# A spectral-filter and MLP block on one core: stores grouped, DRAM copies laid out by block, one bias spread on chip, and a new order of the engines

## The chip, the core and the metric

The kernel runs on one core of a Trainium2 chip. The core has TensorE (PE in the profile; its weight loads are PEld), VectorE (DVE), ScalarE (ACT), GpSimd (POOL) and SyncE (SP), which here issues most of the DMA transfers. Transfers can also be issued from ScalarE's instruction queue. The metric is the device time of one launch in microseconds, as the median of several runs.

## The reference

One block is computed forward and backward in bf16, for 2048 rows of 512 values. The forward pass, cut to what matters:

```
mod = (silu(c) @ w_mod) -> six rows sa, ca, ga, sb, cb, gb
h   = layernorm(x) * (1 + ca) + sa
y   = irfft2( rfft2(h) * (w_r + i w_i) )          # filter of 2048 x 257
x   = x + ga * y
h   = layernorm(x) * (1 + cb) + sb
x   = x + gb * ( relu(h @ w1 + b1)^2 @ w2 + b2 )  # 512 -> 1792 -> 512
```

The kernel returns this x and, for a given grad_out, the gradients of x, w_r, w_i, w1, b1, w2, b2, c and w_mod. In the kernel they are out_0 (x), out_1 (gradient of x), out_2 and out_3 (filter gradients, 2048 x 257), out_4 to out_7 (w1, b1, w2, b2), out_8 (c, 512 values) and out_9 (w_mod).

## The kernel before, in words

The Fourier transforms are matmuls with constant cosine and sine blocks. The launch runs through these stages; the times are those of the profiled execution.

- **0 to 50 us.** x is loaded into x_sb (load_x, four reads of 512 KB), the mod rows are formed (L736), the first layernorm runs (L767 to L784; n1 is stored to n1_dram) and the first transform (L294, L295) is made. As filler, TensorE computes grad_out times w2 transposed (back_products, L840); gT and w2T come by transposing DMAs.
- **50 to 86 us.** The second transform (spec_f23, L318 and L332) gives eight groups gi of the spectrum. Each group is multiplied by the filter (cmul, L415 to L418) and stored to xs_dram for the backward pass. lg_part makes a transposed constant LG out of LF by transposing DMAs. The inverse starts with spec_g1 (L352, L355; its results are evacuated into utcs at L360 on VectorE and L362 on ScalarE).
- **86 to 112 us.** spec_g2 and spec_g3 (L372, evacuated as Tsb at L374; L382) give y row by row. x is loaded again (x1, L911), the second layernorm (from L928 on, L943) gives h2, which a transposing DMA turns into h2T. b2, broadcast to all partitions in grow (L886), goes into x + gb * b2.
- **112 to 265 us.** The MLP, forward and backward, in blocks of rows: L1005 (h), L1034 (its output) and the gradient through them. w1T comes by four transposing DMAs (L1138).
- **265 to 340 us.** The backward spectrum: spec_f23 again, and ew_b, which multiplies by the conjugate filter and, in place in the reloaded xs tile Xb, forms the filter gradient. The filter gradient is stored at L1322 as 34 pieces, those of out_2 from SyncE, those of out_3 from ScalarE. Filler on TensorE are 32 units of the gradient of w1 (grad_w1, L1276; evacuated L1281). GMod.emit (L453 to L474) makes a block of the gradient of w_mod: a matmul (L460), an evacuation gmbc (L462), scaled copies gwm (L469, L471) and their stores (L474). LGb is read back (L1328) and grad_out is read into g_sb (L1341). After that comes the second spec_g1.
- **338 to 412 us.** The second spec_g2 and spec_g3 and the first layernorm's backward (L1421 to L1451) give out_1. Filler are units of the gradient of w2 (grad_w2, L1360; evacuated as gw at L1361, stored at L1362), whose left operands hn are transposing reads of h_dram (L1196). The last mod gradients and out_8 (PE transpose L1484, copy L1486, store L1487) end the launch.

What each engine does, and in which order, is written out by hand: a table ORDER lists for each of the five engines its instructions in the order in which they are to run, and set_order chains them. SyncE's list is thus one queue of DMA issues: an issue whose data or buffer isn't ready holds back all behind it. Every DMA takes one of eight completion semaphores in turn and waits for the transfer that had the semaphore before it, so at most eight are in flight.

SBUF tiles come from pools, and a pool that is opened late takes over memory of one that was released: the tiles of rows (x1, n2rows, y, Tsb) lie where the spectrum tiles Xs were, and the tiles of the last stage where Xb was.

Of the kernel before, what the change touches and what calls it, by code (L numbers as in the profile page):

```python
# [11 lines left out]
FP32 = mybir.dt.float32  # L12
# [6 lines left out]
D = 512  # L19
# [421 lines left out]
class GMod:  # L441
# [7 lines left out]
    def load(self, jc, pool):  # L449
        cs = slice(jc * D, (jc + 1) * D)  # L450
        self.tiles[jc] = [pool.tile([P, 2, D], BF16, name="wmc", bufs=4) for _ in range(2)]
        for dc in range(0, 4, 2):
            self.tc.nc.sync.dma_start(self.tiles[jc][dc // 2], self.wm_view[:, dc:dc + 2, cs])  # L453

    def emit(self, jc, q, row, pool, ppool, nbuf=2, last=False):
# [8 lines left out]
        for dc in range(0, 4, 2):  # L464
            wmc = self.tiles[jc][dc // 2]
            gwm = pool.tile([P, 2, D], BF16, name="gwm", bufs=nbuf)
            for i in range(2):
                if i == 0 or last:
                    nc.scalar.activation(gwm[:, i, :], gmbc, AF.Copy, scale=self.scf[:, dc + i:dc + i + 1])  # L469
                else:  # L470
                    nc.vector.tensor_scalar(gwm[:, i, :], gmbc, self.scf[:, dc + i:dc + i + 1], None, op0=ALU.mult)  # L471
                nc.vector.scalar_tensor_tensor(out=junk, in0=wmc[:, i, :], scalar=K["onef"], in1=gmbc, op0=ALU.mult, op1=ALU.mult,
                                               accum_out=self.gsc[:, jc, dc + i:dc + i + 1])
            nc.sync.dma_start(self.out9_view[:, dc:dc + 2, cs], gwm)  # L474
# [5 lines left out]
        "0-17 106 135-146 18-21 151-154 147-150 159-162 26-27 22-25 28-29 155-158 30-35 167-170 163-166 36-37 175-178 171-174 "  # L480
        "42-43 38-39 44-45 40-41 183-186 179-182 86-89 50-53 187-190 46-49 191-194 107-110 195-198 58-59 54-57 199-202 60-61 "
        "90-93 203-210 62-63 66-69 94-97 64-65 215-218 98-101 211-214 70-73 102-105 74-77 219-222 78-79 111-126 80-85 223-226 303 "
        "127-134 304-311 227-234 312-319 235-238 320-321 324-325 322-323 239-242 328 243-246 326-327 329-331 336-337 332-333 "
        "338-339 334-335 251-254 247-250 340-343 352-353 344 354-355 345-351 255-258 356-359 259-262 360-369 372-373 370-371 "
        "374-391 267-270 448-479 263-266 484-487 480-483 271-278 500-501 488-489 512-515 502-503 279-282 504-505 283-286 490-493 "
        "516-517 494-495 506-511 496-499 287-290 524-525 542-545 530-531 518-519 536-537 526-529 520-521 546-547 522-523 532-533 "
        "548-549 538-539 534-535 540-541 560-565 578-579 550-553 580-583 566-567 554-555 572-575 556-559 568-569 576-577 570-571 "
        "291-294 584-587 295-298 588-592 299-302 593-597 392-395 607-610 606 396-399 652-655 611 400-403 665-668 664 404-407 "
        "678-679 677 680-681 408-415 691-692 416-419 598 690 693-694 420-423 599-604 848 605 424-427 849-850 428-431 851 432-439 "
        "861-862 440-443 695 612 863 613-619 444-447 860 864 620-627 640-643 628-635 882-883 636-639 884-885 644-651 656-663 "  # L490
        "669-676 682-689 696-811 895 812-819 896 820-831 840-847 897 852-859 865-868 898 832-839 873-880 869-872 881 886-894 "
        "900-913 899 1052 914-955 1053 956-983 1054 984-997 1055 998-1023 1065 1024-1027 1064 1028-1031 1066-1068 1032-1035 "
        "1044-1051 1056-1063 1086-1087 1069-1072 1088 1073-1076 1089 1036-1043 1077-1084 1090-1093 1099-1100 1085 1094-1097 1101 "
        "1098 1102 1104-1117 1103 1118-1231 1252 1248-1249 1232-1239 1256-1263 1253 1264-1271 1254 1280-1283 1304-1310 1300-1303 "
        "1296-1299 1255 1250 1284-1287 1240-1247 1288-1295 1326-1332 1276-1277 1315-1321 1278-1279 1337-1343 1251 1348-1354 1272 "
        "1370-1376 1273-1274 1359-1365 1275 1322 1381-1387 1311 1392-1405 1312 1323-1324 1313-1314 1325 1406-1419 1344 1333-1334 "
        "1345-1346 1335-1336 1347 1436-1449 1355 1366 1356 1367 1357-1358 1368-1369 1450-1463 1377 1388-1391 1378-1380 1504-1519 "
        "1420-1421 1424-1425 1422-1423 1426-1429 1432-1435 1430-1431 1464-1487 1537-1552 1520 1488-1489 1500-1501 1490-1492 "
        "1496-1499 1493 1502-1503 1494-1495 1553-1616 1521-1525 1529-1530 1533-1534 1526 1531-1532 1535-1536 1527-1528 1617-1632 "
        "1634-1640 1642-1643 1633 1646-1649 1641 1650-1665 1644-1645 1682-1683 1666-1681 1694-1697 1684-1687 1690-1691 1688-1689 "  # L500
        "1692-1693 1698-1729 1743-1744 1730-1735 1745-1746 1739-1740 1736-1738 1741-1742 1763-1778 1780-1782 1792-1793 1783-1785 "
        "1788-1789 1794-1795 1790-1791 1786 1747-1762 1787 1796-1811 1828 1836-1837 1829 1779 1838-1839 1830-1831 1840-1841 1832 "
        "1842-1843 1833-1835 1812-1827 1864-1867 1860-1863 1868-1885 1890-1891 1886-1889 1896-1899 1892-1895 1914-1915 1900-1903 "
        "1916-1921 1904-1909 1926-1927 1922-1923 1928-1929 1910-1913 1932-1935 1930-1931 1924-1925 1936-1937 1844-1859 1968-1971 "
        "1938-1939 1972-1973 1956-1957 1940-1941 1950-1951 1942-1943 1958-1959 1944-1945 1960-1965 1952-1955 1946-1947 1966-1967 "
        "1974-1975 1948-1949 1976-1979 1984-1985 1980 1986-1987 1981-1983 1988-2004 2006-2008 2005 2010-2013 2009 2014-2029 2048 "
        "2052-2053 2049 2054 2050 2055 2051 2046-2047 2030-2045 2082 2078 2073 2079 2083-2084 2080 2085 2072 2081 2056-2071 2118 "
        "2128 2124 2129 2125-2126 2130 2127 2119 2131 2086-2101 2158 2154 2159 2155-2156 2102-2117 2160 2157 2208-2223 2074-2077 "
        "2120-2123 2150-2153 2149 2161 2132-2148 2200 2162-2177 2201 2204-2206 2202 2194 2203 2195 2207 2178-2193 2224-2240 "
        "2250-2251 2246 2241 2247-2249 2252-2269 2196-2199 2242-2245 2308-2309 2271 2276-2291 2270 2292-2307 2272-2275 2326-2333 "  # L510
        "2310-2325 2350 2334-2349 2367 2351-2366 2368-2416"
    ),
    "ACT": (
        "0 2 1 3 8 5 7 17 4 13 16 6 50 9 51 10 52 20 11-12 53 14 55 54 15 56 19 23-24 57 18 37 42 38 58 21-22 59 27 25 60 26 "
        "30-31 61 44 39 28-29 34 40 62 43 32 41 45 33 63 77 35-36 46 64 79 47 65 80 66 48 81 67 82 84 83 49 68 85-88 69 89-94 "
        "104-107 109 108 70-71 110-111 72-73 113 112 78 74 116 115 114 119 117-118 120 75 121-122 76 123 127 131 130 95 146 132 "
        "150 149 96 124 157 153 97 125 98 126 161 99 160 128 100 129 133 186 101 134-135 102 162 136 103 137-139 190 140-145 "
        "147-148 151-152 197 154 159 158 155-156 163-168 172 169-171 173 178 175 179 174 180-183 176 184-185 177 188 187 189 191 "
        "193 192 198-199 201 200 202 194-196 203 205 204 206-207 209 212 208 211 210 213 226 218 215 219 214 220-222 217 223-224 "
        "230 225 216 227-228 231-232 237 229 233 238-242 234-236 243-244 246 245 247 249 248 251 250 252-253 258 254 259-262 255 "  # L520
        "263 266-267 256 269 257 272 268 265 273 275 274 277 271 264 280-282 270 287 290 283-284 278 291 276 292 279 285-286 "
        "293-294 288-289 295-297 299 298 308 300-301 309 311 303 302 317 304 318 314 319 313 312 320-322 310 323 326 331 305 328 "
        "316 327 332 335 324 334 325 307 306 338 333 340 345 342-343 339 315 344 349 341 354-355 336 348 353 330 337 350 360-361 "
        "329 362 359 366 351 358 367 347 352 346 371-372 357 374 364 363 375 356 373 370 368-369 376 379 377-378 380 365 381-382 "
        "384-385 388 383 389 392 398-399 395 386 394 387 407 404 393 408 403 391 390 402 418 417 396-397 406 411 413 405 414 401 "
        "400 426 412 410 409 440 415 421 427 422-423 416 433 430 432 419-420 431 424 436-437 425 441 429 428 443 442 447 457 "
        "434-435 450 446 452 451 439 438 455 444-445 459 456 448-449 463 458 454 466 453 464 462 467 469 465 472-473 470-471 468 "
        "461 474 460 475-477"
# [1005 lines left out]
```

## Time and profile before

| | |
|---|---|
| median of 3 runs | 412.4 us (410.09 to 412.97) |
| profiled execution, its own time | 415.6 us |
| its span | 413.8 us, mean granted TensorE clock 0.992 |
| TensorE busy | 384.9 us |
| VectorE busy | 342.2 us |
| ScalarE busy | 276.1 us |
| GpSimd busy | 15.3 us |
| DMA | 93.72 MB in 143449 packets, mean 226 GB/s |
| packets under 512 B, under 2 KB | 98225, 129590 |

The profile is of one execution. Busy times don't count the issuing of DMAs nor waits on semaphores. A row of the chain of waits reads: instruction that waited <- what ended the wait, us in total, how often, the longest. A row of a table by stretches of time gives the busy time and, in brackets, the instructions of each engine. Names of tiles are those of the program.

### The profile page before, as it was taken

Reading aid. Unit: us, or ns where it says so; the run is one execution under the profiler, and the core shown is the slowest. Engines: PE = TensorE matmul, PEld = TensorE weight load, DVE = VectorE, ACT = ScalarE, POOL = GpSimd, SP = SyncE. Lnnn points to the kernel's source line nnn. Section 1 sums busy time; section 2 is a strip of 40 time slices with the busy share of each in tenths; the row PEclk is TensorE's granted clock in tenths of the full one; section 3 lists DMA queues with packets and bytes.
Section 4 is the critical chain, followed back from the end, with each engine's and each line's share of the span. In section 5 each row is a group of like instructions: output and inputs, shape, how many; then the busy total and the mean of one; then the engine's idle time right before and its main releaser. Section 6 shows DMA issues by size and latency. Waiting matters only on the chain. (4 is left out here: it accounts for less than half of the span.)

```text
span 413.8 us, 6952 instructions
## 1 busy us (share of the span) xinstructions
PE 384.9 (93%) x2417; PEld 203.2 (49%) x2417; DVE 342.2 (83%) x827; ACT 276.1 (67%) x492; POOL 15.3 (4%) x56
## 2 busy tenths in 40 slices
PE   0699998979999999999999999999998979999985
PEld 0255566645444444444444445455555655444344
DVE  5989879938996789989999999947988918778793
ACT  3459999658972387259526846477565457778794
POOL 5423000000000000000000000000000000000000
PEclk9999999989999999999999999999999989999999
DMA  8999959999399459695988988999999989899996
GB/s 214 200 239 306 264 171 195 326 156 269 112 323 211 124 145 260 140 205 142 246 206 211 197 212 234 260 241 303 273 361 217 217 258 231 162 249 247 261 264 209
DMA packets 143449, 93.72 MB, mean 226 GB/s; under 512 B 98225, under 2 KB 129590, under 8 KB 143158
## 3 DMA queue, kind: packets, MB, share of 16 engines
q1 hardware_dynamic: 140386, 91.63, 89.7%
q10 hardware_dynamic: 3028, 1.65, 1.7%
q8 instruction: 19, 0.31, 0.3%
q14 instruction: 16, 0.13, 0.1%
HBM read 37.52 MB, written 34.24 MB: 173 GB/s over the span
## 5 line engine op out<-in xcount | busy, mean ns | idle before, releaser
L1276 PEld LDWEIGHTS <-h_sb 128*128 128x128 bf16 x256 | 24.6, 98 | 22.4 <-issue 1.3
L840 PEld LDWEIGHTS <-w2T 128*128 128x128 bf16 x224 | 21.9, 101 | 24.8 <-DMA w2T<-in_B_w_dram 4.3
L1034 PEld LDWEIGHTS <-gab 128*128 128x128 bf16 x224 | 21.5, 98 | 25.1 <-issue 0.4
L1005 PEld LDWEIGHTS <-w 128*128 128x128 bf16 x224 | 21.1, 98 | 24.9 <-issue 1.6
L1276 PE MATMUL mm_1s<-gab,h_sb 128*128 128x384 bf16 (+1 forms) x160 | 30.2, 342 | 0.0
L1034 PE MATMUL og_1s<-w1T,gab 128*128 128x512 bf16 x112 | 25.8, 379 | 0.0
L1034 PE MATMUL og_0s<-w1T,gab 128*128 128x512 bf16 x112 | 25.8, 379 | 0.0
L1005 PE MATMUL mm_0s<-h2T,w 128*128 128x512 bf16 x84 | 21.8, 379 | 0.2 <-ACT h2T L982 0.2
L1276 PE MATMUL mm_0s<-gab,h_sb 128*128 128x512 bf16 (+1 forms) x96 | 20.8, 370 | 1.2 <-ACT gmbc L462 1.2
L336 ACT ACTIVATE AE<-psB 128x1024 bf16<-128x1024 f32 x16 | 21.6, 1352 | 0.0
L1005 PE MATMUL mm_1s<-h2T,w 128*128 128x512 bf16 x80 | 20.5, 379 | 0.0
L1360 PE MATMUL mm_0s<-g_sb,hn_0s 128*128 128x512 bf16 x80 | 18.1, 379 | 0.0
L840 PE MATMUL mm_0s<-gT_0s,w2T 128*128 128x512 bf16 x56 | 16.2, 414 | 1.9 <-DMA w2T<-in_B_w_dram 1.3
L1360 PE MATMUL mm_1s<-g_sb,hn_1s 128*128 128x512 bf16 (+1 forms) x80 | 16.4, 358 | 0.0
L840 PE MATMUL mm_1s<-gT_0s,w2T 128*128 128x512 bf16 x56 | 16.1, 415 | 0.0
L372 PEld LDWEIGHTS <-utcs 128*128 128x128 bf16 x128 | 10.8, 101 | 10.5 <-issue 2.3
L1005 PE MATMUL pst<-h2T,w 128*128 128x512 bf16 x60 | 15.4, 379 | 0.0
L840 PE MATMUL mm_0s<-gT_1s,w2T 128*128 128x512 bf16 x56 | 14.4, 379 | 0.0
L840 PE MATMUL mm_1s<-gT_1s,w2T 128*128 128x512 bf16 x56 | 14.4, 379 | 0.0
L1360 PEld LDWEIGHTS <-hn_1s 128*128 128x128 bf16 x96 | 9.3, 98 | 9.4 <-issue 1.8
L407 ACT ACTIVATE inv<-l_mv_1s,eps 128x2 f32<-128x2 f32 x4 | 1.2, 292 | 18.8 <-DVE l_mv_1s L944 18.8
L844 ACT CAST gab<-mm_1s 128x512 bf16<-128x512 f32 x20 | 11.8, 592 | 2.5 <-PE mm_1s L840 2.4
(642 smaller groups left out, 1036.7 us busy)
## 6 DMA issues: line engine op xcount, KB each, us to landing
w<-in_B_w_dram SPq DMA_DIRECT2D x2, 1792.0 KB, 8.2
Z<-wz_dram SPq DMA_DIRECT2D x4, 514.0 KB, 4.8
x_sb<-in_A_x_dram SPq DMA_DIRECT2D x4, 512.0 KB, 5.0
n_dram<-x_sb SPq DMA_DIRECT2D x4, 512.0 KB, 6.6
h_dram<-h2r SPq DMA_DIRECT2D x8, 256.0 KB, 2.3
h_sb<-h_dram SPq DMA_DIRECT2D x1, 2048.0 KB, 8.8
g_sb<-in_grad_out_dram SPq DMA_DIRECT2D x4, 512.0 KB, 6.8
LF_dram<-LF SPq DMA_DIRECT2D x4, 384.0 KB, 2.6
```

The lines of the kernel that those rows point to most:

```text
L336: nc.scalar.activation(dst, ps.rearrange("p r (s e f) -> p (r s) e f", s=2, e=2), AF.Copy, scale=EF_S)
L372: nc.tensor.matmul(ps[:, P * i:P * i + P], lhsT=CS[:, t, i].rearrange("p a b -> p (a b)"), rhs=K["Cf"][:, i, :], start=True, stop=True)
L407: nc.scalar.activation(dst, var, AF.Sqrt, bias=K["eps"])
L840: nc.tensor.matmul(ps, lhsT=w2T[:, dc, fc * P:(fc + 1) * P], rhs=gT[b][:, :, dc, :], start=(dc == 0), stop=(dc == 3))
L844: nc.scalar.copy(out=gaT[b][:, fc, :], in_=ps)
L1005: nc.tensor.matmul(ps, lhsT=w1[:, dc, (fc + i) * P:(fc + i + 1) * P], rhs=h2T[b][:, :, dc, :], start=(dc == 0), stop=(dc == 3))
L1034: nc.tensor.matmul(ps, lhsT=lhs(fc), rhs=rhs[:, fc, :], start=(fc == 0), stop=(fc == NFC - 1))
L1276: nc.tensor.matmul(blocks(ps, fb), lhsT=h2_sb[:, t, dc * P:(dc + 1) * P], rhs=gh_rows(t, fb), start=(t == 0), stop=(t == NT - 1))
L1360: nc.tensor.matmul(ps[:, 0:w], lhsT=hns[fc][:, t, :], rhs=g_sb[:, t, c:c + w], start=(t == 0), stop=(t == NT - 1))
```

## The change

The change consists of these parts.

- GMod.load reads a 512-KB block of w_mod in one transfer, not in two.
- n1_dram, h2_dram, gx1_dram, xs_dram, LF_dram and LG_dram have the block that one transfer moves as their outermost dimension. h2_sb and LGb are read back in four transfers each instead of one.
- x is read in two transfers of eight rows per partition (8 KB per partition, 1 MB) instead of four; grad_out into g_sb likewise.
- lg_part transposes LF from SBUF instead of from LF_dram.
- The spectrum is kept in four tiles of two groups, and stored to xs_dram in four transfers instead of eight.
- b2 is read as one row of 1 KB; a matmul with a row of ones spreads it over the partitions and ScalarE copies it to grow.
- The filter gradients are stored from tiles of four groups, in 18 transfers (six after group 0, six after group 3, six after group 7), all from SyncE. The pool of cmul's temporaries has one buffer of each instead of two.
- out_8 is stored from gcb, 128 partitions of four values, without the PE transpose and the copy.
- All five lists of ORDER are new. Among other things the first mod row stands ahead of the first L840 matmul, two w1T transposes stand ahead of the load of x1 instead of one, and the copies to wz_dram (L1017) stand earlier.

The diff, without the lists of ORDER:

```diff
 class GMod: def load(self, jc, pool):
-        self.tiles[jc] = [pool.tile([P, 2, D], BF16, name="wmc", bufs=4) for _ in range(2)]
-        for dc in range(0, 4, 2):
-            self.tc.nc.sync.dma_start(self.tiles[jc][dc // 2], self.wm_view[:, dc:dc + 2, cs])
+        self.tiles[jc] = pool.tile([P, 4, D], BF16, name="wmc", bufs=2)
+        self.tc.nc.sync.dma_start(self.tiles[jc], self.wm_view[:, :, cs])
...
-    xs_dram = dram.tile([P, 8, 2, 2, FP], BF16, name="xs_dram")
+    xs_dram = dram.tile([4, P, 2, 2, 2, FP], BF16, name="xs_dram")
-    LF_dram = dram.tile([P, 16, 3, P], BF16, name="LF_dram")
+    LF_dram = dram.tile([4, P, 4, 3, P], BF16, name="LF_dram")
...
-    def load_x(q, t, n=4):
+    def load_x(q, t, n=8):
...
     def lg_part(q):
         nc.sync.dma_start(K["LG"][:, 4 * q:4 * q + 4].rearrange("p a y m -> p (a y) m"),
-                          LF_dram[:, 4 * q:4 * q + 4].rearrange("p a y m -> p (a y m)"), transpose=True)
-        nc.sync.dma_start(LG_dram[:, 4 * q:4 * q + 4], K["LG"][:, 4 * q:4 * q + 4])
+                          K["LFall"][:, 4 * q:4 * q + 4].rearrange("p a y m -> p (a y m)"), transpose=True)
+        nc.sync.dma_start(LG_dram[q], K["LG"][:, 4 * q:4 * q + 4])
...
         def dest_f(gi):
-            X = fr.tile([P, 2, 2, FP], BF16, name="Xs")
-            return X
+            if gi % 2 == 0:
+                Xp[0] = fr.tile([P, 2, 2, 2, FP], BF16, name="Xs")
+            return Xp[0][:, :, :, gi % 2, :].rearrange("p i h f -> p h i f")
         def ew_f(gi, X):
             K["cmul"] = cmul(nc, ew, X, Z[gi], Z[gi][:, :, 0, 0:DF], Z[gi][:, :, 1, 0:DF], False)
-            nc.sync.dma_start(xs_dram[:, gi], X)
+            if gi % 2 == 1:
+                nc.sync.dma_start(xs_dram[gi // 2], Xp[0])
...
-    nc.sync.dma_start(grow, B_b2[None, :].broadcast_to([P, D]))
+    nc.sync.dma_start(grow[0:1, :], B_b2[None, :])
+    psb2 = mmps.tile([P, D], FP32, name="mm")
+    nc.tensor.matmul(psb2, lhsT=K["ones_sq"][0:1, :], rhs=grow[0:1, :], start=True, stop=True)
+    nc.scalar.copy(out=grow, in_=psb2)
...
-                nc.sync.dma_start(h2_sb, h2_dram)
+                for k in range(4):
+                    nc.sync.dma_start(h2_sb[:, 4 * k:4 * k + 4, :], h2_dram[k])
...
-    with Slots(tc, name="f23b", bufs=2) as fr, Slots(tc, name="ewb", bufs=2) as ew:
+    with Slots(tc, name="f23b", bufs=2) as fr, Slots(tc, name="ewb", bufs=1) as ew:
...
             for i, o in enumerate((out_2, out_3)):
-                for p0_, n, rows_ in w_parts(o, gi):
-                    K["gW"] = (nc.scalar if i else nc.sync).dma_start(rows_, gW[p0_:p0_ + n, i, :, 0:DF]).ins
+                if gi == 0:
+                    for p0_, n, rows_ in w_parts(o, 0):
+                        K["gW"] = nc.sync.dma_start(rows_, XG[0][p0_:p0_ + n, i, :, 0, :]).ins
+                elif gi % 4 == 3:
+                    a, n = max(gi - 3, 1), min(gi, 4)
+                    v = o.rearrange("(q h g) f -> q h g f", h=2, g=16)
+                    X = XG[gi // 4][:, i, :, a % 4:, :]
+                    K["gW"] = nc.sync.dma_start(v[:, :, a:a + n, :].rearrange("q h g f -> q h (g f)"), X[0:64].rearrange("q h g f -> q h (g f)")).ins
+                    for h in range(2):
+                        K["gW"] = nc.sync.dma_start(v[:, 1 - h, 16 - a:16 - a - n:-1, :], X[64:P, h]).ins
...
-                nc.sync.dma_start(K["LG"], LG_dram)
+                for k in range(4):
+                    nc.sync.dma_start(K["LG"][:, 4 * k:4 * k + 4], LG_dram[k])
...
-                for t in range(0, NT, 4):
-                    K["g_load"] = nc.sync.dma_start(endp["g_sb"][:, t:t + 4, :], g_view[:, t:t + 4, :]).ins
+                for t in range(0, NT, 8):
+                    K["g_load"] = nc.sync.dma_start(endp["g_sb"][:, t:t + 8, :], g_view[:, t:t + 8, :]).ins
...
-        pg = psX.tile([4, P], BF16, name="mm")
-        nc.tensor.transpose(pg, gcb, K["ident"])
-        gcr = fp.tile([4, P], BF16, name="gcr", bufs=1)
-        nc.vector.tensor_copy(gcr, pg)
-        nc.sync.dma_start(out_8.rearrange("b (dc p) -> (b dc) p", p=P), gcr)
+        with nc.allow_non_contiguous_dma(reason="512 values"):
+            nc.sync.dma_start(out_8.rearrange("b (dc p) -> p (b dc)", p=P), gcb)
```

## The prediction

> **What bounds the kernel now.** I read the busy times first, then the stretches of 10 us, then the chain of waits in those stretches where TensorE is not full.
>
> ```profile
> PE 384.9 (93%) x2417; PEld 203.2 (49%) x2417; DVE 342.2 (83%) x827; ACT 276.1 (67%) x492; POOL 15.3 (4%) x56
> ```
>
> TensorE bounds the kernel: 28.9 us of the 413.8 us span are left to it, so what its idle stretches give back is all that this change can win.
>
> ```profile
> 0.00:10.00 10.00, 0.56 (x7) 0.35 (x8) 5.19 (x33) 3.83 (x6) 5.19 (x34) 1.00 0.85 212
> 10.00:20.00 10.00, 7.26 (x33) 2.64 (x31) 9.26 (x38) 4.49 (x8) 4.54 (x12) 1.00 1.17 197
> ...
> 90.00:100.00 10.00, 8.94 (x50) 4.73 (x51) 5.02 (x12) 7.76 (x16) 0.00 (x0) 0.83 0.87 246
> ...
> 330.00:340.00 10.00, 7.26 (x62) 5.61 (x61) 1.77 (x4) 4.53 (x10) 0.00 (x0) 0.83 0.86 230
> ...
> 400.00:410.00 10.00, 8.38 (x60) 5.68 (x60) 6.70 (x17) 7.33 (x13) 0.00 (x0) 1.00 0.89 282
> ```
>
> The columns are the stretch, its length, busy us of PE, PEld, DVE, ACT and POOL, the granted clock, the DMA share and GB/s. From 112 to 260 us PE is busy 10.00 of 10 in every row: nothing can be won there. The idle time lies at the start (12.2 us up to 20), around 90 (3.0 in 80 to 100), at 310 to 340 (4.0) and after 390 (5.7). In two rows the clock is 0.83: for 3.4 us matmuls of 512 columns started every 0.43 us, not 0.216, which cost 1.7 us each beside the gap.
>
> ```profile
> PE mm_0s L840 <- DMA w2T<-in_B_w_dram: 1.3, 1, 1.3
> ...
> PE psY L382 <- ACT Tsb_0s L374: 2.9, 1, 2.9
> ...
> PE psG_3s L352 <- ACT utcs L362: 2.1, 1, 2.1
> PE mm_0s L1276 <- ACT gmbc L462: 1.2, 1, 1.2
> ...
> PE mm_0s L1360 <- ACT gw_0s L1361: 1.6, 1, 1.6
> PE mm_1s L1360 <- DMA hn_3s<-h_dram: 0.7, 1, 0.7
> ```
>
> Behind each stands a transfer, which ScalarE's own waits show:
>
> ```profile
> ACT Tsb_0s L374 <- DMA xs_dram<-Xs_1s: 3.6, 1, 3.6
> ...
> ACT gmbc L462 <- DMA out_dram<-Xb_1s: 3.2, 1, 3.2
> ...
> ACT utcs L362 <- DMA out_dram<-Xb_2s: 1.9, 1, 1.9
> ...
> ACT gw_0s L1361 <- DMA out_dram<-gw_0s: 1.8, 1, 1.8
> ```
>
> The 2nd and 3rd are no data: ScalarE itself issues half of the filter-gradient stores, an issue waits for one of eight transfer slots, and the evacuations behind it wait too.
>
> **The change part by part,** against the profiled run (415.6 us, 413.8 of it span; 0.8% above the median of 412.4).
>
> *Start, 0 to 22 us.* x comes in 1-MB reads, wm_0s is SyncE's 2nd transfer instead of its 7th, and the first mod row and the first psA matmuls run before most of L840. PE waited 1.48 us for the second w2T at 19.7 and 0.54 before the mod row. Work of about 1 us is moved into those waits: -1.0. Ends: both go (-2.0); up to 512 KB more ahead of gT_0, at the 244 GB/s of 80 to 85 us, delay it (+2.1).
>
> *50 to 76 us.* The L318/L332 work is the same; ACT is busy 10.00 of 10 from 50 to 70. Four xs stores of 514 KB replace eight, and the lg transposes (6.3 and 4.8 us to landing) no longer wait for LF_dram. 0; ends: the three gaps of 0.78, 0.76 and 0.37 go (-1.9), or as much is added.
>
> *76 to 112 us.* Tsb_0s (L374) waits until the last xs store lands, since its tile takes over Xs's memory: issued 81.90, landed 90.3. It stays the last store, now 514 KB, behind much the same backlog, so the 3.1-us gap stays. What is new: x1_0s was issued behind one w1T transpose (issued 82.43, 6.45 us of SyncE), and is now behind two (the second took 8.40). From 81.9 that gives an issue at 94.8 to 97.3 instead of 90.67; landing 4.0 later, 98.8 to 101.3; layernorm (L943) needed it at 97.66. Queued behind L943 is the chain to h2T, which PE reached with all its fillers spent (wait 0.38 at 111.7), so 1.1 to 3.6 us would show in full. Against it, the wz copies and grow (128 KB) no longer stand there. The b2 row adds one matmul (0.2) and one ACT copy (0.6, the L844 row's 592 ns) where ACT is busy 9.91 of 10. I take +1.5, near the low end, because SyncE should reach the first w1T a little sooner. Ends: the gap and its half clock shrink (-2); two issues of 8.40, another half-clock window and b2 (5.4 + 1.7 + 0.6 = +7.7).
>
> *112 to 265 us.* Block-laid copies, h2_sb in 4 parts (one took 8.8 us): hidden by a full PE. 0, up to +1 if h2_sb's parts come late.
>
> *265 to 345 us.* The 34 filter-gradient stores become 18, none on ACT: 17 issues of about 0.58 us (9.9 us) and the waits of 3.2 and 1.9 leave ACT. PE's gaps of 1.37 (314.4), 2.23 (330.3), 0.84 (337.0) and 1.7 of half clock are 6.1 us. Next late is Tsb_0s of the second g2: it waits until all six stores of gi 4 to 7 have landed. Before, the last product ended at 328.5, the last store was issued at 333.08, and landings held Tsb_0s until 339.54, hidden by a w1 unit; psY ran at 340.45. Now six issues of 0.6 us follow the last product, and 1.03 MB at 230 to 270 GB/s is 3.8 to 4.5 us: landing near 336, psY at about 337. That is -3.5, not -6.1. Ends: all 6.1 go; or the last lands 9.38 us after its issue at 333 (the slowest row here, LGb), psY at 343: +2.6.
>
> *Tail.* PE's 0.52, 0.90, 1.79 (405.3) and 0.32 are 3.5 us:
>
> ```profile
> 389.74 6.49 DMA hn_3s<-h_dram
> ...
> 401.61 4.83 DMA out_dram<-gw_0s
> ```
>
> In the new order hn transposes go out earlier, a grad_w2 unit (3.5 us) stands between the column sums and the last mod-gradient matmul, and a gw tile is written again about 13 us after its store instead of 5. -2.5; ends -3.5 and +1.
>
> *out_8.* The PE transpose and the DVE copy (0.1 us each) go; 512 runs of 2 bytes go straight to DRAM, a form that no row shows. By the nearest rows, the 1-KB gcr store and Z's 32-KB reads of 514-byte runs (3.1), it lands in 1.6 to 5 us. After gcb one grad_w2 unit of 16 matmuls is still to run (1.76 us for the last one here), then its copy (0.37) and the last gw store (1.60), 3.7 us of cover: 0; ends -0.2 and +2. The Trainium skill, "DMA: Bandwidth & Descriptors", section "Rules for kernel authors", speaks against it: a non-contiguous last dim becomes one descriptor per element. It gives no time for 512 of them; the sum stays as it is.
>
> On the clock: the rows of 0.83 followed idle gaps of 3.1 and 2.2 us, while gaps of 1.4 and 1.8 were followed by 1.00. The Trainium skill, "TensorE: Matmul & The Clock Gate", section "HAM oscillation — how this bites in real kernels", says to keep idle gaps under about 3.4 us. By it the 2.2-us gap should have cost nothing and 1.7 us less would be there to win; the trace shows the loss, so the row decides.
>
> Sum: -1.0 + 0 + 1.5 + 0 - 3.5 - 2.5 + 0 = -5.5: a profiled run of 410.1 us. Scaled by 412.4/415.6, the median is **406.9**.
>
> **Rivals.**
> *SyncE's single queue gives it back (slower).* Place: x1_0s behind two w1T issues. For: 8 slots, issues of 8.40 us, fillers spent at 111.7. Against: h2T has other work in its chain. Price +7.7 instead of +1.5: the sum is +0.7, 413 us; if the gi 4-to-7 stores are held in the same queue too (+2.6 for -3.5), it is +6.8, 419 us. It decides from a loss of 7.0 us on: with the half clock and b2 in it, x1_0s landing past about 102.4.
> *The gaps only move (within 1%).* Without the ACT issues PE reaches L382 sooner and waits for the landings there, and the tail waits for other tiles: -1 in all, 411.4. For: Tsb_0s waited 2.18 us for landings already. Against: the stores start at once after the last product.
> *All is covered (faster).* x1_0s in time, 6.1 and 3.5 gone: -1.0 - 1.9 - 6.1 - 3.5 = -12.5, 400 us. Against: DVE, which sets the last product, is busy 9.93 in 320 to 330.
> *The change doesn't do what it says:* excluded for the stores, as the issue lists show 18 on SyncE and one small store left on ACT.
>
> **Numbers.** Forecast 0.45 (own range 402 to 411); covered 0.18; gaps move 0.14; slower rival 0.23. About 1% is what a measurement here tells from no change, so the borders are 408.3 and 416.5. Faster: 0.18 + 0.32 of the forecast = 0.50. Within 1%: 0.13 + 0.14 + 0.05 of the rival = 0.32. Slower: 0.18. The range 399 to 418 leaves out about a tenth at each end.
>
> **What would show it.** No ACT wait on an out_dram<-Xb store, PE full from 310 to 330, and the first psY of the second g2 at its old place less 3 us: the main term is right. A PE gap above 2 us just before h2T's first L1005, with x1_0s landing after 99: the rival. A wait on hn or gw after 390 over 1 us: the tail term is wrong. Wrong altogether if idle time appears between 112 and 260, or the clock row falls to 0.83 more than twice.

## The result and the profile after

The changed kernel takes 424.63 us (median of 4 runs, 422.3 to 427.78) against 412.69 us of the kernel before: 1.0305 of it, 95% interval 1.0237 to 1.0374. The forecast was 406.9. The profiled execution took 424.7 us, 422.9 of it span, at a mean clock of 0.974.

The busy times of the changed kernel, on its page:

```profile
PE 382.3 (90%) x2417; PEld 201.3 (48%) x2417; DVE 342.7 (81%) x826; ACT 276.7 (65%) x493; POOL 14.4 (3%) x56
```

The engines have about as much to do as before: TensorE 382.3 us (384.9 before), VectorE 342.7 (342.2), ScalarE 276.7 (276.1). Yet the span is 9.1 us longer. Where that lies is seen in the stretches of the changed kernel (columns as in the prediction):

```profile
0.00:10.00 10.00, 0.45 (x2) 0.31 (x3) 5.93 (x25) 4.31 (x8) 5.59 (x35) 1.00 0.88 260
10.00:20.00 10.00, 6.93 (x41) 3.15 (x40) 9.54 (x38) 5.29 (x9) 4.16 (x10) 1.00 1.03 217
...
90.00:100.00 10.00, 9.70 (x64) 4.96 (x63) 9.38 (x22) 9.60 (x19) 0.00 (x0) 1.00 1.02 248
...
330.00:340.00 10.00, 4.66 (x24) 2.40 (x22) 1.44 (x4) 3.53 (x7) 0.00 (x0) 0.66 1.01 228
...
400.00:410.00 10.00, 5.65 (x49) 4.61 (x49) 4.90 (x14) 4.86 (x10) 0.00 (x0) 0.89 0.67 201
410.00:420.00 10.00, 0.00 (x0) 0.00 (x0) 0.00 (x0) 0.00 (x0) 0.00 (x0) 0.50 0.02 0
420.00:422.90 2.90, 0.00 (x0) 0.00 (x0) 0.00 (x0) 0.00 (x0) 0.00 (x0) 0.50 0.00 0
```

From 410 us to the end no engine works at all, and the transfer engines move next to nothing (busy for 0.02 of the time). The last matmul of the last grad_w2 unit starts at 405.4 us; in the kernel before it was 410.5. So the arithmetic ended 5.1 us sooner, nearly what the sum said, and 16 us were then spent waiting for stores. The list of DMA issues after 402 us (columns: size, us from issue to landing) names them:

```profile
out_dram<-gwm_3s SPq DMA_DIRECT2D x1, 256.0 KB, 9.1
...
out_dram<-gw SPq DMA_DIRECT2D x1, 64.0 KB, 16.1
out_dram<-gw ACTq DMA_DIRECT2D x1, 64.0 KB
out_dram<-gcb_0s SPq DMA_DIRECT2D x1, 1.0 KB
```

A 64-KB store of gw, issued at 405.71, lands at 421.8. Right ahead of it, at 405.25, stands the new store of out_8. The 256-KB store of gwm issued one microsecond ahead of that, at 404.29, is late too: it lands after 9.1 us.

The second thing that has changed is the place of TensorE's waits. Its own waits, and one of ScalarE's, in the changed kernel:

```profile
PE mm_1s L837 <- DMA w2T<-in_B_w_dram: 1.9, 1, 1.9
...
PE psY L382 <- ACT Tsb_0s L374: 1.0, 1, 1.0
...
PE psY_0s L382 <- DMA g_sb<-in_grad_out_dram: 5.3, 1, 5.3
...
PE mm_1s L1378 <- ACT gw_0s L1379: 1.0, 1, 1.0
...
ACT Tsb_0s L374 <- DMA out_dram<-Xb_1s: 5.6, 1, 5.6
```

The waits at 314, 330 and 337 us are gone. In their place is one of 5.3 us at the first psY of the second g2, and in 330 to 340 us the clock is 0.66. The row names g_sb, which landed last; what psY needs is Tsb_0s, and that waited for the last stores of the filter gradient (out_dram<-Xb_1s), issued from 322.4 to 326.8 and landed by 335.0.

Five marks on TensorE divide the launch: A the first matmul on AE (L318), B the first on h2T (L1005), C the last on w1T (L1034), D the first psY of the second g2, E the last of grad_w2. In us, with three of the experiments told below:

| | 0 to A | A to B | B to C | C to D | D to E | E |
|---|---|---|---|---|---|---|
| before, the profiled execution | 55.5 | 55.7 | 140.3 | 89.5 | 69.5 | 410.5 |
| e2_before_direct (order of before) | 55.4 | 51.6 | 140.4 | 90.3 | 69.4 | 407.1 |
| e6_before_sp (order of before but for stores in C to D) | 55.4 | 52.0 | 140.3 | 89.4 | 70.8 | 407.9 |
| changed kernel | 53.2 | 53.9 | 140.7 | 87.9 | 69.7 | 405.4 |
| e1_transposed (changed, out_8 as before) | 52.1 | 54.3 | 140.7 | 87.5 | 68.9 | 403.5 |

The row of before was an unlucky execution: A to B took 55.7 us, with the gap of 2.9 in front of psY and the half clock at 88 to 94 us, and 51.6 and 52.0 in two other profiles with the same order there.

The marks do not cut the work at quite the same place. In the new order 100 of the 224 matmuls of back_products (L840 in the kernel before) stand ahead of A, 104 before, so four matmuls of 512 columns, 0.9 us, have moved behind A. About 0.4 us of small matmuls has moved from behind C to ahead of it. D to E holds the same 411 matmuls in all five (the rows below also count those that overlap an edge).

The stretches C to D and D to E in the kernel before, in the changed kernel and in e1 (columns as above):

```profile
251.50:341.00 89.50, 84.75 (x645) 50.90 (x644) 69.11 (x156) 53.04 (x88) 0.00 (x0) 0.98 0.97 263
341.00:410.50 69.50, 66.45 (x413) 33.95 (x411) 56.06 (x128) 54.30 (x109) 0.00 (x0) 1.00 0.99 238
```

```profile
247.80:335.70 87.90, 82.18 (x637) 49.16 (x636) 69.94 (x154) 50.14 (x84) 0.00 (x0) 0.98 1.00 274
335.70:405.40 69.70, 67.88 (x412) 34.69 (x411) 54.39 (x126) 54.88 (x110) 0.00 (x0) 0.97 1.00 238
```

```profile
247.10:334.60 87.50, 82.12 (x638) 49.13 (x637) 69.89 (x154) 50.12 (x84) 0.00 (x0) 1.00 0.99 272
334.60:403.50 68.90, 67.65 (x412) 34.52 (x411) 54.39 (x126) 54.84 (x110) 0.00 (x0) 0.98 0.97 241
```

### The profile page after: what moved, and what is told of

Read it like the earlier page. It is cut to its first block, busy times and chain, and to the rows that moved or that the text cites. A ratio compares the mean times of both kernels' runs of the same rounds, so it can differ in the third digit from the quotient of the medians.

```text
span 422.9 us, 6929 instructions
## 1 busy us (share of the span) xinstructions
PE 382.3 (90%) x2417; PEld 201.3 (48%) x2417; DVE 342.7 (81%) x826; ACT 276.7 (65%) x493; POOL 14.4 (3%) x56
## 4 chain that ended last, share of the span: by engine, by line
PE 62%; DVE 11%; DMA 9%; SPq 8%; ACT 4%; issue 2%; ACTq 0%; DVEq 0%
PE og_0s L1038 9%; PE og_1s L1038 9%; PE mm_0s L1281 5%; PE mm_1s L1378 5%; PE mm_1s L1009 4%; PE mm_0s L1009 4%; PE mm_1s L837 3%; PE mm_1s L1281 3%; PE mm_0s L1378 3%; PE mm_0s L837 3%; PE pst L1009 3%; DMA xs_dram<-Xs_3s 2%; SPq L692 2%; SPq L689 2%; DMA g_sb<-in_grad_out_dram 2%
## 5 line engine op out<-in xcount | busy, mean ns | idle before, releaser
L1281 PE MATMUL mm_0s<-gab,h_sb 128*128 128x384 bf16 (+1 forms) x160 | 30.2, 342 | 0.0
L1281 PE MATMUL mm_1s<-gab,h_sb 128*128 128x512 bf16 (+1 forms) x96 | 21.9, 384 | 0.0
L1009 PE MATMUL mm_1s<-h2T,w 128*128 128x512 bf16 x84 | 21.6, 379 | 0.0
L1009 PE MATMUL mm_0s<-h2T,w 128*128 128x512 bf16 x80 | 20.5, 379 | 0.0
L1378 PE MATMUL mm_1s<-g_sb,hn_0s 128*128 128x512 bf16 x80 | 18.1, 379 | 1.3 <-ACT gw_0s L1379 1.0
L1378 PE MATMUL mm_0s<-g_sb,hn_1s 128*128 128x512 bf16 (+1 forms) x80 | 16.4, 358 | 0.0
L837 PE MATMUL mm_1s<-gT_0s,w2T 128*128 128x512 bf16 x56 | 14.4, 379 | 1.9 <-DMA w2T<-in_B_w_dram 1.9
L837 PE MATMUL mm_0s<-gT_0s,w2T 128*128 128x512 bf16 x56 | 15.2, 395 | 0.5 <-DMA w2T<-in_B_w_dram 0.5
L1378 PEld LDWEIGHTS <-hn_0s 128*128 128x128 bf16 x80 | 7.7, 97 | 10.6 <-issue 1.9
```

Source lines behind the costliest of these rows:

```text
L837: nc.tensor.matmul(ps, lhsT=w2T[:, dc, fc * P:(fc + 1) * P], rhs=gT[b][:, :, dc, :], start=(dc == 0), stop=(dc == 3))
L1009: nc.tensor.matmul(ps, lhsT=w1[:, dc, (fc + i) * P:(fc + i + 1) * P], rhs=h2T[b][:, :, dc, :], start=(dc == 0), stop=(dc == 3))
L1281: nc.tensor.matmul(blocks(ps, fb), lhsT=h2_sb[:, t, dc * P:(dc + 1) * P], rhs=gh_rows(t, fb), start=(t == 0), stop=(t == NT - 1))
L1378: nc.tensor.matmul(ps[:, 0:w], lhsT=hns[fc][:, t, :], rhs=g_sb[:, t, c:c + w], start=(t == 0), stop=(t == NT - 1))
```

## Experiments

### The store of out_8

Two theories: the direct store costs the 15 us by itself; or the end is held by something that the new order put there. e1 undoes that part in the changed kernel:

```diff
-        with nc.allow_non_contiguous_dma(reason="512 values"):
-            nc.sync.dma_start(out_8.rearrange("b (dc p) -> p (b dc)", p=P), gcb)
+        pg = psX.tile([4, P], BF16, name="mm")
+        nc.tensor.transpose(pg, gcb, K["ident"])
+        gcr = fp.tile([4, P], BF16, name="gcr", bufs=1)
+        nc.vector.tensor_copy(gcr, pg)
+        nc.sync.dma_start(out_8.rearrange("b (dc p) -> (b dc) p", p=P), gcr)
```

> The changed kernel with out_8 stored as before: PE transpose of gcb, copy, one row store, last on SyncE. In the changed kernel's profile the last matmul starts at 405.4 us (410.5 before) and the span ends at 422.9, with every engine idle from 406.5. Theory: the direct store of 512 two-byte values costs all of that. Then the last store lands about 2 us after the last matmul and the span is about 408, the time 408 to 410, 0.985 to 0.995 of before. Rival (the end is held by something else, such as the two last gw stores or the SyncE queue): the span stays above 418.

Measured: 410.8 us against 412.56, 0.9978 of before (0.9938 to 1.0018). The profiled execution took 408.51 us, with a span of 406.7, and in it the store of gwm lands after 2.4 us:

```profile
out_dram<-gwm_3s SPq DMA_DIRECT2D x1, 256.0 KB, 2.4
```

e2 is the mirror image, the same diff the other way round in the kernel before:

> The kernel before with that part of the change alone: out_8 stored from gcb, no transpose, no copy; all else and all orders as before. Theory that the store costs 14 to 16 us wherever it stands last: its issue comes about 2 us earlier than the old one, the span ends near 425, time 1.025 to 1.035 of before. Rival (it is slow only together with what the new order puts beside it): within 1% of before.

Measured: 427.0 us, 1.0374 of before (1.0306 to 1.0442), span 424.6. Here the store's own landing is on record, in the list of DMA issues after 402 us of e2:

```profile
out_dram<-gw ACTq DMA_DIRECT2D x1, 64.0 KB, 15.8
out_dram<-gcb_0s SPq DMA_DIRECT2D x1, 1.0 KB, 15.9
```

So the store of 1 KB takes 15.9 us, in either order, and the store issued behind it lands with it. That settles the loss: without this part the changed kernel can't be told from the one before; with it alone the kernel before is as slow as the changed one.

What makes it slow? Its 512 runs of two bytes, or where they fall? e3 has a quarter of the writes, four times as long; e4 the same writes, each in 64 bytes of its own:

```diff
-            nc.sync.dma_start(out_8.rearrange("b (dc p) -> p (b dc)", p=P), gcb)
+            nc.sync.dma_start(out_8.rearrange("b (p dc) -> p (b dc)", p=P), gcb)   # e3
+            nc.sync.dma_start(far_dram[:, :, 0], gcb)      # e4; far_dram is [P, 4, 32] in bf16
```

> The changed kernel, out_8 stored from gcb as 128 runs of 8 bytes instead of 512 of 2 (the 512 values stand in another order in out_8). If each short write costs the same, 128 cost a quarter: 15 us become about 4, the span is about 411. If the cost is one of the transfer as a whole, the span stays near 422. If it is one of writes under 4 bytes alone, the span is near 408.

> The changed kernel, the 512 two-byte writes go to a scratch area where each has 64 bytes for itself, so none shares 64 bytes with another (out_8 is left out). If the cost comes from writes that fall into the same 64 bytes and are done one after the other, it goes: span near 408. If each two-byte write costs the same wherever it falls, the span stays near 422.

Measured, one run each: spans of 411.0 (e3) and 409.4 us (e4), against 420.5 to 426.0 in the runs of the changed kernel and 406.5 to 411.8 in those of e1. The gw store issued on SyncE right behind out_8's, in e3 and then in e4:

```profile
out_dram<-gw SPq DMA_DIRECT2D x1, 64.0 KB, 4.7
```

```profile
out_dram<-gw SPq DMA_DIRECT2D x1, 64.0 KB, 2.4
```

It lands 16.1 us after its issue in the changed kernel, 4.7 behind 128 writes of 8 bytes, 2.4 behind 512 writes of two bytes that lie apart. e3 came out where a cost for each write had put it; e4 shows that neither the length of the writes nor their number is the cost by itself. It appears where many short writes lie side by side, 32 of them in each 64 bytes of out_8, and nearly all of it is gone where each has its own 64. e4 also writes to another DRAM buffer than out_8; that the buffer makes the difference was not tested, but in e1, where rows are stored into out_8, the launch ends 3.2 us after mark E. In what unit they get in each other's way, a stretch of 64 bytes, a larger one, or the 1 KB as a whole, was not measured. In e2 it is 15.9 us less the 1.6 us that the last gw store took in the kernel before, 14.3 us for 512 writes, or 28 ns each, as if done one after the other. The same sum for e3, 4.7 less 1.6 us for 128 writes, gives 24 ns each. Both are estimates. The transfer engines are not what is slow: the packet records of the changed kernel have the 512 packets of two bytes taken up within 0.45 us (406.18 to 406.62), in 7 to 9 ns each.

### Where the other gain went

The prediction's main term was that the gaps at 314, 330 and 337 us come from stores issued by ScalarE. e6 changes only that in the kernel before:

```diff
-                    K["gW"] = (nc.scalar if i else nc.sync).dma_start(rows_, gW[p0_:p0_ + n, i, :, 0:DF]).ins
+                    K["gW"] = nc.sync.dma_start(rows_, gW[p0_:p0_ + n, i, :, 0:DF]).ins
```

> The kernel before, its 17 filter-gradient stores of out_3 issued by SyncE right behind their twins of out_2 instead of by ScalarE; nothing else is changed. The prediction's main term says that the issues on ScalarE cause the gaps at 314, 330 and 337 us and 1.7 us of half clock: they shrink, the time is 2 to 5 us below before, 0.988 to 0.995. Rival (the gaps only move, because the transfers still take as long to land, now with 34 issues of 0.6 us in one queue): 0.998 to 1.01.

Measured: 413.58 us against 412.25, 1.003 of before (0.9995 to 1.0065). The rival holds. The chain of waits of e6 from 320 to 345 us:

```profile
ACT Tsb_0s L374 <- DMA out_dram<-Xb_2s: 7.1, 1, 7.1
PE psY_0s L382 <- ACT Tsb_0s L374: 4.9, 1, 4.9
```

ScalarE is free of the issues, spec_g1 runs through, and TensorE then stands 4.9 us in front of psY, for the same landings. In e1 it is the same; one wait of TensorE there, and two stretches:

```profile
PE psY_0s L382 <- DMA g_sb<-in_grad_out_dram: 5.0, 1, 5.0
```

```profile
320.00:330.00 10.00, 9.60 (x94) 7.07 (x92) 7.76 (x12) 4.08 (x9) 0.00 (x0) 1.00 1.07 216
330.00:340.00 10.00, 5.42 (x24) 2.65 (x25) 2.90 (x6) 3.53 (x7) 0.00 (x0) 0.83 0.94 255
```

The transfer engines are full (share 1.07) while they move 216 GB/s. Four edits of e1 ask what holds the landings back, and what fills the gap. e5 moves a 1-MB read from right behind the stores:

```diff
 SyncE: six filter-gradient stores of groups 4 to 7
-SyncE: g_sb, second 1-MB read
 SyncE: store of gw1, load of n1, load of n1
+SyncE: g_sb, second 1-MB read
 SyncE: hn transposes
```

> As e1_transposed, and SyncE issues the second 1-MB read of g_sb behind the two loads of n1 instead of right behind the six filter-gradient stores of groups 4 to 7. In e1_transposed those stores were issued from 321.4 to 325.8 us, the second g_sb read at 325.9, and the first psY of the second g2 ran only at 334.6, after a TensorE gap of 5.1 us and 1.7 us of half clock. Theory: the two 1-MB reads around the stores share the transfer engines with them, so that they land 8.5 us after their issue, not 4. With the second read behind them they land near 331, psY comes at 330 to 332, and the time falls by 3 to 5 us: 406 to 408, 0.985 to 0.990 of before. Rival (the stores themselves are slow, 514-byte runs written backwards): psY stays at 334 to 335 and the time at 410 to 411.

Measured: 410.86 us against 412.25, 0.9979 (0.9948 to 1.0011), the rival's time. From the first matmul of spec_g1 (L352) to psY it is 17.0 us instead of 18.7, but what is won is waited for elsewhere, by TensorE in front of the second psY and by VectorE for g_sb. TensorE's waits of e5 from 320 us on, and one of VectorE's:

```profile
PE psY_0s L382 <- ACT Tsb_0s L374: 2.7, 1, 2.7
PE psY_1s L382 <- ACT gs_1s L1450: 0.8, 1, 0.8
...
DVE g_sb L1402 <- DMA g_sb<-in_grad_out_dram: 4.1, 2, 3.2
```

e8 leaves all transfers alone and moves a unit of matmuls into the gap:

```diff
 TensorE: w1 unit (384 columns), psT of the first pair
+TensorE: w1 unit (16 matmuls of 512 columns)
 TensorE: psY_0s, psT, psY_1s, psT
-TensorE: w1 unit (16 matmuls of 512 columns)
```

> As e1_transposed, and on TensorE one unit of the w1 gradient (16 matmuls of 512 columns, 3.45 us) that stood behind the first psY matmuls of the second g2 stands ahead of them, in the gap of 5.0 us in which TensorE waits for the last filter-gradient stores to land; no transfer is moved. Theory: the gap is where the gain of the rest of the change went, since nothing stands on TensorE to fill it. The gap falls to about 1.5 us, the 1.7 us of half clock go, the time falls by 3.5 to 5 us: 406 to 408, 0.983 to 0.990 of before. Rival (the chain through Tsb, VectorE and the final rows sets the time from there on, and TensorE then waits as long behind it): 410 to 411, as e1_transposed.

Measured: 409.73 us against 410.86, 0.9963 (0.9934 to 0.9993). Against e1's 0.9978 that is about 0.6 us where 3.5 to 5 were expected, and the intervals overlap: near the rival, "as e1_transposed". In e8's profile, TensorE's waits from 320 us on and one stretch:

```profile
PE psY_0s L382 <- DMA out_dram<-gw_2s: 2.2, 1, 2.2
PE psT_1s L372 <- ACT Tsb_3s L374: 1.4, 1, 1.4
```

```profile
340.00:350.00 10.00, 8.96 (x50) 4.92 (x50) 8.61 (x19) 8.95 (x19) 0.00 (x0) 0.78 1.02 211
```

The unit was missing where it was taken from (1.4), and the gap of 2.2 that was left still brought half clock, for 6.8 us. But two other runs of e8 have a mean clock of 1.000 and took 410.72 and 408.83 us, against 410.96 at 0.987 for this one: half clock alone does not set the time. e10 puts both edits together with that of e7 (below):

> e9_unit_x with the second g_sb read behind the two n1 loads, as in e5_g_late. In e8_unit_early a gap of 2.4 us was left in front of psY, which put TensorE on half clock for 6.8 us; in e5_g_late the stores landed some 1.7 us sooner after the start of spec_g1. If the two add, the gap is below 1 us, no half-clock stretch follows, and the time is 405 to 407, 0.985 to 0.991 of before. Rival: the later g_sb read holds up VectorE's scaling (4.1 us of wait in e5_g_late) and takes it back: 408 to 409, as e9_unit_x.

Measured: 410.97 us against 412.31, 0.9978 (0.9944 to 1.0012). They don't add: in e10's profile the gap in front of the first psY is gone, but gaps of 1.6 and 1.8 us follow it, at 333 and 341 us. e11 asks whether the short runs of the stores count:

```diff
-                        K["gW"] = nc.sync.dma_start(v[:, 1 - h, 16 - a:16 - a - n:-1, :], X[64:P, h]).ins
+                        if gi == 7:
+                            K["gW"] = nc.sync.dma_start(far_dram[i, h], X[64:P, h].rearrange("q g f -> q (g f)")).ins
+                        else:
+                            K["gW"] = nc.sync.dma_start(v[:, 1 - h, 16 - a:16 - a - n:-1, :], X[64:P, h]).ins
```

> As e1_transposed, but of the six last filter-gradient stores the four that write single rows of 514 bytes backwards write the same bytes as runs of 2056 bytes to a scratch area (these rows are left out of out_2 and out_3). If the short runs make these stores land 8.5 us after their issue, the first psY of the second g2 comes at 331 or sooner instead of 334.6, and the time falls by 3 us or more, 0.985 to 0.991 of before. If it is the amount of traffic of that stretch, whatever the runs, psY stays within 1 us and the time at 0.995 to 1.0.

Measured: 406.54 us against 412.31, 0.9861 (0.981 to 0.9912), against 0.9978 for e1. The same two stretches of e11:

```profile
320.00:330.00 10.00, 9.69 (x89) 6.74 (x87) 7.66 (x13) 4.61 (x10) 0.00 (x0) 1.00 0.94 238
330.00:340.00 10.00, 7.15 (x52) 4.23 (x53) 5.18 (x9) 5.48 (x11) 0.00 (x0) 1.00 0.91 255
```

With the same bytes in runs four times as long, the transfer engines are less busy (0.94) and move more (238 GB/s). psY comes 17.1 us after the first L352, not 18.7: less than half of what was expected there. But all four runs of e11 have a mean clock of 1.000, where the ten of e1 have 0.988 to 0.996: the gap fell into pieces of 1.3 and 1.9 us, and no half clock followed. The median clock of e1, 0.9915, is a loss of 3.5 us in 409, so by this estimate clock can be up to 3.5 of the 4.8 us between the two ratios. That it is so much is not shown: e12 below, with 0.996 to 1.000, gains only 1.4 us, and the two profiles of e1 and e11 differ by 0.6 us of span. What this edit alone brought is more than any change of order. It also turned the rows of the four stores forwards and sent them to another buffer, so that the length of the runs is the likely cause, not the only one possible.

Last, the wait itself. Tsb waits for stores whose memory it does not use: its tile lies over the first Xb tile, but a pool is given back as a whole. e12 gives each Xb tile a pool, at the same addresses:

```diff
-    with Slots(tc, name="f23b", bufs=2) as fr, Slots(tc, name="ewb", bufs=1) as ew:
+    with Slots(tc, name="f23b", bufs=1) as fr, Slots(tc, name="f23c", bufs=1) as fr2, Slots(tc, name="ewb", bufs=1) as ew:
...
-                Xt[0] = fr.tile([P, 2, 2, 4, FP], BF16, name="Xb", bufs=2)
+                Xt[0] = (fr2 if g else fr).tile([P, 2, 2, 4, FP], BF16, name=f"Xb{g}")
```

> As e1_transposed, but the two Xb tiles come from two pools at the same addresses. The tiles of the final rows (Tsb, gs, n1 and others) lie over the first Xb tile and not over the second; with one pool, Tsb waits for the stores from both. Now it waits for the stores of groups 0 to 3 alone, which have landed long before. No instruction is moved. Theory: the wait of psY for the stores of groups 4 to 7 is where the gain of the rest of the change went; the gap of 5.0 us and the half clock behind it go, psY runs near 330, and the time is 405 to 407, 0.982 to 0.990 of before. Rival (the same stores still hold up the loads of n1 and the hn transposes behind them on SyncE, and VectorE or TensorE waits there instead): 409 to 411.

Measured: 409.3 us against 411.9, 0.9944 (0.9911 to 0.9976). psY runs at 330.7 instead of 334.6 and the clock stays full, as expected; but E comes at 403.1 instead of 403.5 us in these two profiles. TensorE's waits of e12 from 320 us on, and its stretches:

```profile
PE psY_1s L382 <- ACT gs_1s L1450: 2.1, 1, 2.1
PE mm_1s L1380 <- ACT gw_2s L1381: 1.3, 1, 1.3
...
PE psY_0s L382 <- ACT Tsb_0s L374: 0.5, 1, 0.5
```

```profile
330.00:340.00 10.00, 8.63 (x61) 4.92 (x59) 3.56 (x7) 5.71 (x12) 0.00 (x0) 1.00 1.08 240
340.00:350.00 10.00, 8.59 (x64) 4.18 (x66) 9.26 (x24) 8.90 (x19) 0.00 (x0) 1.00 1.05 211
350.00:360.00 10.00, 9.04 (x47) 4.19 (x47) 5.34 (x13) 6.12 (x13) 0.00 (x0) 1.00 1.12 263
```

In place of 5.0 us in front of psY, TensorE waits 0.5 us there and 2.1 and 1.3 us behind it. (The busy times are lower bounds: 24 of e12's 2418 matmuls have no record.) The transfer engines are still full (1.08, 1.05, 1.12). So what was won by taking the wait away was mostly given back behind it: 0.9944 against 0.9978 is 1.4 us, near the rival's 409 to 411.

### The start

e7 is e1 with the second 1-MB read of x behind the second w2T transpose, e9 the same in e8, e13 in e12:

```diff
 SyncE: x (1 MB), wm_0s, gT_0, w2T (first)
-SyncE: x (second 1 MB)
 SyncE: w2T (second)
+SyncE: x (second 1 MB)
```

> As e1_transposed, and the second 1-MB read of x is issued behind the second w2T transpose instead of ahead of it. In the changed kernel's profile TensorE waits 2.05 us for that w2T at 18.1 us, in e1_transposed 0.74. If the 1 MB ahead of it makes that wait, it falls below 0.5 us, unless x then arrives late for the layernorm and the same time is lost at the psA matmuls behind it.

> As e8_unit_early, and the second 1-MB read of x is issued behind the second w2T transpose. If the 1 to 2.5 us that TensorE waits for that w2T in most profiles of the new order come from that read ahead of it, this is 0.5 to 1.5 us faster than e8_unit_early; if x then comes late, the same or slower.

> As e12_two_pools, and the second 1-MB read of x issued behind the second w2T transpose. e9_unit_x against e8_unit_early (0.995 and 0.9963) left open whether that read costs anything: if it does, this is 0.5 to 1.5 us below e12_two_pools; if not, the same within 0.5 us.

Measured: e7, one run, 409.12 us; the wait in front of that matmul is 0.6 us in its profile and in e1's, so this doesn't decide. e9: 408.88 us against 410.86, 0.995 (0.9922 to 0.9978), where e8 had 0.9963. e13: 408.47 us against 411.9, 0.9923 (0.9893 to 0.9954), where e12 had 0.9944. Both times the later read is 0.8 us faster, but the intervals overlap; that it costs anything is likely, not shown, and not by the wait that was named: at that place TensorE waits 1.4 us in e8's profile and 2.1 in e9's, 1.5 in e12's and 1.1 in e13's, and mark A comes no sooner with the later read (52.8 and 53.1 us in e8 and e9, 52.5 in e12 and e13). e13 beats both kernels, by 0.8% the one before.

## Why the prediction was wrong

- **out_8: the step that failed.** It was costed at 0, ends -0.2 and +2, because "by the nearest rows", runs of 514 bytes, it would land in 1.6 to 5 us under 3.7 us of cover. It took 15.9 us. The change of sign and three quarters of the miss come from this term: the forecast was 0.9867 of before, and it is 0.9978 without the term, 1.0305 with it. Rows of long runs were no bound for 512 writes of two bytes into 1 KB; with nothing to compare with, the upper end should have been open, and the forecast's own range with it. The rule of the Trainium skill that the prediction weighed, "DMA: Bandwidth & Descriptors", section "Rules for kernel authors", pointed at the right line: one descriptor for each element, and the packet records do show 512 of two bytes. It does not give the cost, and e4, with as many descriptors and 0.8 us of cost at most (2.4 less 1.6), shows that the count isn't it. The same page's section "Specifications" says that transfers under 512 bytes are written by read-modify-write; e4 is under it as well. What the runs point to is that the writes lie side by side.
- **Filter-gradient stores, 265 to 345 us: sized -3.5, measured -1.6 to -2.8** (C to D, 87.9 and 87.5 against 89.5 and 90.3), of which 0.4 is work that moved ahead of C. The waits on ScalarE went as said, and the next late thing was the one named, Tsb_0s. Its size was off: the last landing was put 7.5 us behind the last product (six issues of 0.6 us, then 1.03 MB in 3.8 to 4.5 us) and came 11.7 us behind it (323.3 to 335.0); the fifth of the six stores took 8.6 us from its issue. In e11 and in e5 it took 7.3 and 7.2, against 8.5 in e1: the short runs and the 1-MB read beside them may each be a part, and the rest is open. Three waits became one, and TensorE's idle time in C to D did not fall: 4.8 us before, 5.7 in the changed kernel, 5.4 in e1. e6 shows that moving the issues off ScalarE gains nothing by itself. Here the second rival, "the gaps only move", was right.
- **Tail: sized -2.5, measured about 0** (D to E, 68.9 to 69.7 against 69.4 to 70.8). The waits on hn_3s (0.7) and on gw (1.6) fell, but others of 1.0 and less stand in that stretch: TensorE's idle time in it went from 3.05 us to 1.82 in the changed kernel and 1.25 in e1, less than the 2.5 that were counted on. And half clock, which followed the new gap in front of psY, now lies in this stretch, for 3.9 and 3.4 us, which cost about half of that and took the gain back. e12 shows the same from another side: a gap removed early comes back later while the transfer engines are full.
- **Start: sized -1.0, measured -2.3 to -3.4** (0 to A), of which 0.9 is the four matmuls that moved behind A.
- **76 to 112 us: sized +1.5.** Against the usual A to B (51.6, 52.0) the new order needs 1.9 to 2.7 us more, but not for the reason given. x1_0s was issued at 87.6 us in the changed kernel and not at 94.8 to 97.3, since SyncE reached the first w1T at 78.5 and the second took 3.8 us. The first rival, built on this, did not happen. The four matmuls from ahead of A (0.9) and the matmul of b2 (0.2) are 1.1 of the difference; where the rest comes from was not tested.
- **112 to 265 us: sized 0, measured +0.4** (B to C), as much as the matmuls that moved ahead of C.
- **The base.** The sum was made against one execution, 415.6 us, and scaled. Its gap at 88 us is no property of the order: two other profiles with the same order lack it. Against those (407.1 and 407.9), E of the changed kernel came 1.7 to 2.5 us sooner, not 5.1, and against the median e1 gains 0.9 us with an interval from -2.6 to +0.7. That the sum of -5.5 came near the profile's -5.1 at E was luck: by stretch the profile has -2.3, -1.8, +0.4, -1.6 and +0.2, where the sum had -1.0, +1.5, 0, -3.5 and -2.5.

## What to carry to other kernels

A transfer in a form that no row shows has no upper bound from other rows: measure it alone before it goes to the end of a kernel, where nothing covers it, and do not let neighbouring partitions write single values next to each other into DRAM unmeasured; a TensorE transpose, a copy and one store in rows, as in e1, avoid it. Where transfers fill a stretch, taking a wait off an engine moves the gap to the next thing that needs a landing; longer runs gave more here than any order did. And take more than one profile of the kernel before, or find out which of its gaps come back, before pricing them.

## What the runs showed of the hardware

- A store of 512 times two bytes into 1 KB of DRAM lands 15.9 us after its issue (e2), about 28 ns a write, and the store behind lands with it; 64 bytes apart, in another buffer, the store behind lands after 2.4 us (e4). A 256-KB store issued 1 us ahead of it lands after 9.1 us (changed kernel) instead of 2.4 (e1). The transfer engines hand the 512 packets on in 0.45 us.
- With the same bytes in runs of 2056 instead of 514 bytes, forwards and into another buffer, four stores in one stretch made the whole kernel 1.2% faster (0.9861 against 0.9978).
- TensorE fell to half clock, for 3.4 or 6.8 us, after gaps of 2.1 and 2.9 us (before), 2.2 (e8), 2.7 (e5) and 5.0 (e1), and in e10 after one of 1.6 us. It kept full clock in e11 with gaps of 1.3 and 1.9 us less than a microsecond apart, in e12 after one of 2.1 and in e9 after one of 2.3 us, so no single length divides the two.
